# Phase weight loaded by SyncE, two-token loads for five groups, seven block products in two pairs instead of three, and another order of steps

## The chip, the cores and the metric

The kernel runs on one core of a Trainium2 chip. The metric is the device time of one execution in microseconds (us). TensorE (PE) multiplies and transposes, VectorE (DVE) and ScalarE (ACT) move and change what PE wrote, GpSimd (POOL) and SyncE (SP) mostly start DMA transfers.

## The reference, cut to what matters

q, k and v are (8, 8, 576, 64): batch, heads, tokens, head dimension. Attention is local to chunks of 64 tokens. Its output x (8, 576, 512) goes through a mixing layer with four weights.

```python
def _attn_ref(q, k, v):
    ...                                   # chunks of 64 tokens
    scores = scale * np.matmul(q_c, k_c.transpose(0, 1, 2, 4, 3))
    ...
    attn = np.exp(scores)
    attn = attn / (np.sum(attn, axis=-1, keepdims=True) + 1e-09)
    out = np.matmul(attn, v_c)

def _moe_ref(x, w_theta, w_tok_r, w_tok_i, w_ch):
    theta = x @ w_theta
    cos_t, sin_t = (np.cos(theta), np.sin(theta))
    zr = x * cos_t
    zi = x * sin_t
    yr = np.einsum('ts,bsd->btd', w_tok_r, zr)
    yi = np.einsum('ts,bsd->btd', w_tok_i, zi)
    y = yr + yi
    u = x + y
    return (u + np.maximum(u @ w_ch, 0.0)).astype(np.float32)
```

## The kernel before, in words

The batches are taken two at a time, as pairs 0 to 3. The 2 x 576 tokens of a pair are nine tiles of 128, in five groups: A and B hold the first 512 tokens of the pair's first batch (two tiles each), C and D those of its second, and M is one tile with the last 64 tokens of both.

Nothing is scheduled by a program. `ORDER` is a list of steps, and each engine does its instructions in the order of that list. A step reads `kind.pairGroup.bank`: `H.0D.2` is the projection of group D of pair 0 into PSUM bank 2. A digit at the end of a kind is a half of the step (one tile of two, or one half of the heads); halves 2 and 3 are halves of the columns of the first tile. The kinds that matter here:

- `qF`, `kF` (line 181): POOL's load of q or k, cast to fp16, four tokens to a partition, so 64 partitions hold a group. `q`, `k` (lines 194 and 208): two tokens to a partition for a group of two tiles, 128 partitions; plain rows for M. `v` (lines 222, 232): v, in two or three transfers.
- `lt`, `lc`, `lw` (lines 251, 254, 243): the phase weight w_theta, the channel weight w_ch, and the token weights in parts.
- `F` (line 301, 128 transposes of 64x64), `FL` (line 316, 32 transposes of 128 columns), `L` (line 339, 32 of 128 columns for a group of two tiles), `N` (line 335): PE transposes q and k. `tq`, `tk` copy them to SBUF (`V` and `A` in these and other names: by VectorE or ScalarE).
- `S` scores, `e` exp, `V` attention times v, `n` normalisation (lines 405, 422, 440, 452 and 454): x of a group.
- `X`, `Q` (lines 478, 487): transposes of x; `xA`, `xV` their copy; `H` (line 518): x times w_theta; `g` cos and sin; `z` the products zr and zi on VectorE.
- `TW`, `tw`: transposes of the token weights and their copy.
- `Y` (lines 590, 604): token mixing done directly. A group of a batch takes nine products to a tile. `YA` to `YM` do the part of it that comes from one group. `y` (line 723) adds x and makes u.
- `K` (line 693) with `j` (line 653) and `r` (line 712): token mixing of A to D of both batches by seven block products in place of eight. `j` takes differences of z on VectorE, `jw` sums of the weight blocks; `r` adds a product from PSUM to x, eight times for a pair.
- `U`, `R`, `uA`, `uV`, `W` (line 518 again), `w` (line 733), `s`, `sA`: u is transposed, copied, multiplied by w_ch, relu and u are added, and the result is stored by SyncE's or ScalarE's queue.
- `D` fills PE at the start with products of zeros; `pe`, `pg` load ScalarE's table for exp or sine.

Pair 0 uses `Y` (its parts by group), pairs 1 to 3 use `K` for A to D and `Y` for M. Loads of pairs 1 to 3 pass `gate`: POOL waits until the latest normalisation named before them in `ORDER` has run. The q and k tiles, the token weights, the differences of z and the later output tiles share one pool of ten buffers (`nat`).

Of the kernel before, what the change touches and what calls it, by code (L numbers as in the profile page):

```python
# [9 lines left out]
FP32 = mybir.dt.float32  # L10
# [12 lines left out]
n0.0C n1.0C H1.0A.7 H0.0A.6 v.0B V1.0B.0 n1.0B v.0M lw.02 Q.0C.4 xA.0C g1.0A V0.0M.2 n0.0M g0.0A
V0.0B.0 V1.0M.3 H.0C.4 lw.00 qF.1C kF.1C n0.0B X0.0B.0 n1.0M qF.1A kF.1A X1.0B.1 z.0D xV1.0B
Q.0M.2 xA.0M qF.1B kF.1B v.1C TW.02.6 twV.02 H.0M.3 g.0C TW.03.1 twA.03 q.1M k.1M xV0.0B z1.0A
z.0C H1.0B.0 v.1A g.0M z0.0A qF.2A v.1D TW.01.6 twV.01 H0.0B.1 g0.0B z.0M TW.00.4 F.1C.3.2 tq.1C
twA.00 jw.00 YD.0D.6 g1.0B z1.0B YC.0D.6 F.1A.0.1 tkA.1C S.1C.2 pe.00 e.1C YM.0C.4 tq.1A YM.0D.6
y.0D YC.0C.4 tkA.1A z0.0B F.1B.0.1 qF.1D kF.1D V0.1C.2 v.1B S.1A.6 lw.04 tq.1B YD.0C.4 e.1A y.0C
n0.1C kF.2A lc.00 tkA.1B YA.0A.6 V1.1A.0 n1.1A V0.1A.4 YB.0A.6 v.1M V1.1C.0 n0.1A S.1B.2 L.1M.4
qF.2C e.1B X.1A.5 qF.2D xA.1A n1.1C X.1C.0 kF.2C YM.0A.6 U.0D.1 H.1A.2 xV.1C pg.00 g.1A tq.1M  # L30
uV.0D H.1C.0 tkV.1M kF.2D F.1D.5.4 tkA.1D y.0A jw.01 v.2A R.0C.6 g.1C tq.1D uV.0C YA.0B.2 S.1D.4
V0.1B.6 YM.0B.2 n0.1B z.1C YB.0B.2 e.1D y.0B FL.2A.0 qF.2B tqA.2A V1.1D.6 q.2M V0.1D.4 n0.1D
W.0D.2 S.1M.4 k.2M n1.1D w.0D X.1D.6 kF.2B TW.04.7 tkA.2A e.1M v.2D twV.04 V1.1M.0 V0.1M.1
S.2A.2 xA.1D e.2A V1.1B.4 n1.1B n0.1M z.1A H.1D.6 n1.1M X.1B.5 pg.00 g.1D xV.1B W.0C.2 w.0C
ja.1C R.0A.0 X.1M.4 uA.0A sA.0C z.1D qF.3A jc.1D U.0B.5 H.1B.6 uA.0B v.2C g.1B xA.1M W.0A.0
Ka.1A.2 w.0A F.2C.4.5 F.2D.0.1 ra.1A tq.2D tkA.2C tkA.2D sA.0D jb.1D qF.3D Y.0M.7 V0.2A.0 n0.2A
z.1B tqA.2C H.1M.6 y.0M N.2M.4 tkA.2M g.1M Kf.1C.2 S.2D.0 tqA.2M F.2B.7.6 V1.2A.4 rc.1C n1.2A
z.1M v.3D e.2D tqA.2B kF.3D Kg.1D.2 rg.1B X.2A.0 xV.2A Ke.1C.4 re.1D tkA.2B v.2M Km.1D.2 qF.3B
U.0M.1 rf.1D H.2A.6 pg.00 g.2A uV.0M Kc.1D.4 jd.1B S.2C.0 pe.00 e.2C q.3M v.2B s.0A rd.1C
V0.2D.6 n0.2D Y.1M.2 S.2B.6 kF.3A y.1M V0.2C.0 n0.2C e.2B k.3M Kb.1B.4 z.2A V1.2C.6 qF.3C kF.3C  # L40
S.2M.0 e.2M n1.2C W.0B.2 rb.1A V1.2D.0 n1.2D Q.2C.6 W.0M.4 U.1C.5 w.0B s.0B v.3A w.0M U.1A.0
uV.1C X.2D.1 xA.2C H.2C.2 xV.2D V1.2M.4 V0.2B.6 uA.1A V0.2M.5 pg.00 g.2C n1.2M n0.2B H.2D.0
W.1A.6 g.2D n0.2M Q.2M.4 xA.2M F.3A.2.3 F.3D.0.1 z.2C w.1A V1.2B.4 n1.2B tkA.3D W.1C.6 tqA.3A
ja.2C z.2D X.2B.1 w.1C H.2M.2 xA.2B Kd.1B.4 tkA.3A tqA.3D g.2M H.2B.6 rh.1B v.3C s.0M S.3A.0
jb.2D kF.3B R.1D.2 Ka.2A.4 g.2B v.3B Ke.2C.6 z.2M uA.1D ra.2A Kf.2C.4 F.3C.2.3 e.3A V0.3A.0
jc.2D tkA.3C re.2D n0.3A tqA.3C rc.2C Kc.2D.6 rd.2C V1.3A.0 n1.3A S.3D.2 e.3D Kg.2D.4 z.2B rg.2B
S.3C.6 s.1A e.3C Q.3A.0 W.1D.2 U.1B.6 v.3M Km.2D.4 xA.3A H.3A.0 w.1D rf.2D V0.3C.2 n0.3C R.1M.4
uV.1M uA.1B W.1B.6 sA.1C jd.2B F.3B.2.3 N.3M.4 pg.00 g.3A z.3A w.1B Kb.2B.0 tqA.3B tkA.3B
V1.3C.2 tqA.3M rb.2A S.3B.6 pe.00 e.3B Y.2M.5 n1.3C tkV.3M Q.3C.0 xA.3C V0.3D.6 y.2M n0.3D
S.3M.2 W.1M.4 e.3M w.1M U.2C.5 uA.2C V1.3D.0 V1.3M.2 n1.3D s.1B V0.3M.3 n0.3M n1.3M H.3C.6 pg.00  # L50
g.3C V0.3B.0 sA.1M Q.3D.4 xV.3D Kd.2B.2 n0.3B rh.2B V1.3B.0 n1.3B R.2D.6 uA.2D W.2C.4 w.2C
Q.3B.0 xV.3B R.2B.6 z.3C uA.2B H.3D.2 g.3D R.2A.0 ja.3C uA.2A Q.3M.6 xA.3M z.3D jb.3D H.3B.4
# [9 lines left out]
def kernel(  # L62
# [22 lines left out]
    GT = 2 * P  # L85
# [20 lines left out]
    nat = ctx.enter_context(tc.tile_pool(name="nat", bufs=10))  # L106
# [60 lines left out]
    def gate(p):  # L167

        if p and marks:
            nc.gpsimd.tensor_copy(out=seen, in_=marks.pop())  # L170
            marks.clear()

    def load_qk(p, g, which, plain, f=None):
        j0, bb, s0 = GROUPS[g]
        gate(p)
        if (p, g) not in nats:
            nats[p, g] = nat.tile([P, 2, 2 * DM], FP16, name="qk16", tag="nat")
        if plain is None:
# [560 lines left out]
    def store(p, g, f, queue):  # L739
# [71 lines left out]
    with tc.manual_schedule():  # L811
        for step in ORDER:
# [5 lines left out]
            p, g = int(at[0]), int(at[1]) if at[1].isdigit() else at[1]  # L818
# [36 lines left out]
```

## Time and profile before

| | us |
|---|---|
| time, median of 3 runs | 203.94 (202.31 to 204.08) |
| the profiled execution: time | 205.1 |
| the profiled execution: span | 203.3 |
| PE busy | 186.4 (92%) |
| VectorE busy | 150.3 (74%) |
| ScalarE busy | 124.4 (61%) |
| POOL busy, mostly starting transfers | 83.3 (41%) |
| last matmul ends | 197.9 |
| mean granted PE clock | 0.999 |

The span runs from the first to the last instruction of the profiled execution; its time is 1.8 us longer. Matmuls overlap in PE's pipeline, so a group's mean (380 ns for a 128x512 matmul) isn't what one of them adds to the time: in the chain of waits eight of them take about 1.8 us.

### The profile page before, as it was taken

The page shows a single profiled execution, that of the slowest core. Times are in us where ns is not written, and L with a number is a line of the kernel's source. Part 1 is how long each engine was busy: PE and PEld are TensorE (multiplying, and loading weights), DVE is VectorE, ACT ScalarE, POOL GpSimd, SP SyncE. Part 2 cuts the span into 40 slices and gives each one's busy share as a digit, 9 for nine tenths or more (in the row PEclk, how much of TensorE's full clock was granted, in tenths as well). Part 3 has the DMA queues.
Part 4 walks back from the last instruction along what each step waited for, and adds up shares of the span by engine and source line. Part 5 has one row for each costly group of instructions (what it writes and reads, how often), then busy time and mean ns, then how long its engine had stood idle before and what let it go on. Part 6 is the DMA issues. An engine that isn't in the chain of part 4 may idle for free.

```text
span 203.3 us, 7900 instructions
## 1 busy us (share of the span) xinstructions
PE 186.4 (92%) x3567; PEld 99.6 (49%) x3567; DVE 150.3 (74%) x238; ACT 124.4 (61%) x150; POOL 83.3 (41%) x134
## 2 busy tenths in 40 slices
PE   7677587999989979999999999999999999999990
PEld 2345445555455545555455564455555544445530
DVE  0042738975766869989988888979988899889480
ACT  2354577995168869679673978956889366001510
POOL 7875957749959675105956137002000000000000
PEclk9999999999999999999999999999999999999999
DMA  5999999999999999962999929505121002004875
GB/s 62 177 191 146 157 141 196 195 175 121 167 178 182 175 128 104 221 223 23 136 141 129 228 108 124 34 3 77 59 106 41 19 3 103 0 0 157 298 286 194
DMA packets 70433, 26.48 MB, mean 130 GB/s; under 512 B 47232, under 2 KB 65792, under 8 KB 70400
## 3 DMA queue, kind: packets, MB, share of 16 engines
q0 software_dynamic: 65408, 16.54, 85.9%
q10 hardware_dynamic: 2496, 4.72, 6.5%
q1 hardware_dynamic: 2496, 4.72, 6.4%
q8 instruction: 28, 0.46, 0.9%
q14 instruction: 5, 0.04, 0.1%
HBM read 33.06 MB, written 9.44 MB: 209 GB/s over the span
## 4 chain that ended last, share of the span: by engine, by line
PE 84%; DMA 4%; POOL 3%; issue 3%; ACT 2%; DVE 1%; ACTq 0%; POOLq 0%
PE ps L518 32%; PE ps L693 21%; PE ps L604 8%; DMA qk<-in_k_dram 4%; PE ps L590 4%; PE ps L478 4%; PE ps L440 3%; PE ps L301 3%; PE ps L487 3%; PE ps L405 3%; POOL qk L181 2%; PE ps L269 2%; POOL v L232 1%; ACT kT L372 1%; PE ps L316 1%
## 5 line engine op out<-in xcount | busy, mean ns | idle before, releaser
L232 POOL DMA_DIRECT2D v<-in_v_dram x48 | 36.3, 778 | 3.6 <-DMA qk<-in_k_dram 2.0
L518 PE MATMUL ps<-wch,uT 128*128 128x512 f16 x144 | 34.1, 380 | 1.2 <-issue 1.2
L518 PE MATMUL ps<-wtheta,xT 128*128 128x512 f16 x144 | 34.5, 380 | 0.0
L712 DVE TENSOR_TENSOR x<-ps,x 128x1024 f16<-128x1024 f32 x24 | 29.1, 1221 | 4.6 <-PE ps L693 4.1
L501 ACT COPY uT<-ps 128x1024 f16<-128x1024 f16 (+1 forms) x14 | 13.6, 982 | 25.8 <-PE ps L487 18.7
L733 DVE SCALAR_TENSOR_TENSOR o<-ps,x 128x1024 f32<-128x1024 f32 (+1 forms) x20 | 22.2, 1115 | 6.7 <-PE ps L518 6.4
L454 DVE TENSOR_TENSOR x<-ps,recip 128x512 f16<-128x512 f32 (+1 forms) x40 | 25.5, 638 | 1.4
L532 ACT ACTIVATE cos<-ps,pihalf 128x1024 f16<-128x1024 f32 (+1 forms) x22 | 21.1, 959 | 6.8 <-PE ps L518 5.8
L422 ACT ACTIVATE eT<-ps 128x1024 f16<-128x1024 f32 (+1 forms) x18 | 16.5, 926 | 11.5 <-PE ps L405 11.2
L372 ACT COPY kT<-ps 128x1024 f16<-128x1024 f16 (+1 forms) x18 | 16.3, 922 | 9.6 <-PE ps L301 5.5
L518 PEld LDWEIGHTS <-uT 128*128 128x128 f16 x144 | 13.1, 98 | 16.2 <-issue 1.7
L518 PEld LDWEIGHTS <-xT 128*128 128x128 f16 x144 | 12.9, 98 | 13.6
L536 ACT ACTIVATE sin<-ps 128x1024 f16<-128x1024 f32 (+1 forms) x22 | 19.0, 865 | 0.0
L693 PE MATMUL ps<-z,wT 128*128 128x512 f16 x72 | 18.8, 379 | 0.0
L170 POOL COPY seen<-recip 1x1 f32<-1x1 f32 x16 | 3.2, 199 | 37.4 <-DVE recip L452 37.4
L452 DVE RECIPROCAL recip<-ps 128x8 f32<-128x8 f32 (+1 forms) x40 | 7.9, 198 | 12.7 <-PE ps L440 11.9
L604 PE MATMUL ps<-z,wT 128*128 128x512 f16 x72 | 16.9, 380 | 0.1
L368 DVE COPY qT<-ps 128x1024 f16<-128x1024 f16 (+2 forms) x11 | 6.4, 581 | 14.3 <-PE ps L316 9.3
L693 PE MATMUL ps<-zsum,wsum 128*128 128x512 f16 x72 | 16.7, 379 | 0.2 <-DVE x L712 0.2
L693 PEld LDWEIGHTS <-wsum 128*128 128x128 f16 x96 | 9.1, 98 | 10.5 <-issue 0.2
L693 PEld LDWEIGHTS <-wT 128*128 128x128 f16 x96 | 9.1, 98 | 10.3
L370 ACT COPY qT<-ps 128x1024 f16<-128x1024 f16 (+2 forms) x12 | 9.9, 823 | 6.5 <-PE ps L316 5.8
(68 smaller groups left out, 294.3 us busy)
## 6 DMA issues: line engine op xcount, KB each, us to landing
qk<-in_q_dram POOLq DMA_DIRECT2D x16, 256.0 KB, 6.0
qk<-in_k_dram POOLq DMA_DIRECT2D x16, 256.0 KB, 6.7
out_dram<-o ACTq DMA_DIRECT2D x8, 512.0 KB, 4.9
out_dram<-o SPq DMA_DIRECT2D x8, 512.0 KB, 3.7
v<-in_v_dram POOLq DMA_DIRECT2D x40, 64.0 KB, 5.3
v<-in_v_dram POOLq DMA_DIRECT2D x16, 128.0 KB, 5.7
wnat<-in_moe_w_tok_r_dram POOLq DMA_DIRECT2D x2, 288.0 KB, 5.8
wnat<-in_moe_w_tok_i_dram POOLq DMA_DIRECT2D x2, 288.0 KB, 6.3
```

The source lines that it names most:

```text
L232: nc.gpsimd.dma_start(v16[rows, slot + tile, :, 0:D], v[2 * p + bb, :, t0 : t0 + m, :].rearrange("h s d -> s h d"),)
L372: nc.scalar.copy(out=t.rearrange("p x s c -> p x (s c)").rearrange("p x (c s) -> p x c s", s=n), in_=ps.rearrange("p x s c -> p x c s"),)
L422: nc.scalar.activation(out=eT.rearrange("p h r e c -> p (h r e) c"), in_=ps, func=AF.Exp, scale=scale)
L454: nc.vector.tensor_tensor(out=tokens(p, g, "x")[:, :, f * NE * D : (f + 1) * NE * D].rearrange("p c (h d) -> p c h d", h=NE), in0=psv[:, 0 ...
L501: (nc.vector.tensor_copy if how == "V" else nc.scalar.copy)(out=to.rearrange("p b (r c) -> p b r c", c=CH), in_=psv)
L518: nc.tensor.matmul(ps[:, a * DM : a * DM + cols.stop - cols.start], xT[:, b0 + a, db, :], weight[:, db, cols], start=(db == 0), stop=(db = ...
L532: nc.scalar.activation(out=cos[:, 0:n].rearrange("p a e -> p (a e)"), in_=pin, func=AF.Sin, bias=pihalf, scale=1.0,)
L536: nc.scalar.activation(out=sin[:, 0:n].rearrange("p a e -> p (a e)"), in_=pin, func=AF.Sin)
L604: nc.tensor.matmul(ps[:, a * DM : a * DM + DM], wT[:, kt, t0 : t0 + P], zs[bb], start=(done + k == 0), stop=(done + k == NK - 1),)
L693: nc.tensor.matmul(ps[:, a * DM : a * DM + DM], wt, zt, start=fresh and i == 0, stop=i == len(terms) - 1, skip_group_check=to in ("x", "z"),)
L712: nc.vector.tensor_tensor(out=u, in0=st[p]["ps_k", frm], in1=u, op=ALU.add)
L733: nc.vector.scalar_tensor_tensor(out=o, in0=ps[:, 0 : n * m].rearrange("p (j d) -> p j d", j=n), scalar=0.0, in1=u, op0=ALU.max, op1=ALU.add,)
```

## The change

The phase weight is loaded in two fp32 halves by SyncE's queue and cast to fp16 by VectorE (`ctV`, new), instead of one casting load by POOL. Both halves use buffers of the pool `nat`. Groups B, A, C, D of pair 0 and A of pair 1 are loaded with two tokens to a partition (`q`, `k`) and transposed by `L`, for 0B and 0A in halves; M is transposed by `N`. Pairs 1 and 2 use the seven block products; pair 3 uses `Y`, its groups C and D a tile at a time. The order of nearly all steps is another: it begins with 0B, 0M and 0A (the first batch of pair 0), the direct token mixing of that batch begins before group D is transposed, and the last tile of all goes through `W`, `w` and the store in two halves of 256 columns.

```diff
@@ ORDER, cut to the beginning and the end @@
-qF.0A kF.0A id.00 init.00 D.12.0 qF.0D D.5.0 FL1.0A.0 kF.0D FL0.0A.2 tqA1.0A tq0.0A tkA1.0A
-S1.0A.0 tkA0.0A F.0D.7.6 tq.0D tkA.0D D.5.2 S.0D.2 e1.0A S0.0A.4 e0.0A v.0A qF.0C D.2.0 V0.0A.0
-qF.0B V1.0A.4 n0.0A kF.0B D.6.0 FL0.0B.0 e.0D FL1.0B.2 kF.0C F.0C.6.7 tkA0.0B tqA0.0B n1.0A
-X1.0A.4 tkA.0C tq1.0B v.0D X0.0A.5 D.3.0 V0.0D.0 tq.0C q.0M k.0M n0.0D lt.00 xV0.0A tkA1.0B
-S1.0B.2 V1.0D.6 n1.0D e1.0B S.0C.0 L0.0M.2 L1.0M.3 e.0C tkV0.0M tkV1.0M X.0D.5 xV.0D tq1.0M
-tqA0.0M S0.0B.0 e0.0B S0.0M.6 S1.0M.0 e1.0M H.0D.2 xV1.0A e0.0M v.0C V0.0C.0 V1.0C.4 pg.00 g.0D
...
-uA.3B sA.1D U.3M.4 uA.3D W.3D.2 s.3A w.3D W.3B.0 sA.3C R.2M.2 sA.3D uV.3M w.3B s.3B W.3M.4 w.3M
-s.3M uA.2M W.2M.7 w.2M sA.2M
+q.0B k.0B init.00 D.12.0 lt.00 ctV1.00 ctV0.00 q.0M k.0M id.00 D.15.0 L0.0B.0.1 tkA0.0B
+L1.0B.7.6 tq1.0B N0.0M.1 tkV0.0M tkA1.0B q.0A N1.0M.2 tq0.0B S1.0B.6 tkV1.0M tq0.0M S0.0M.0
+e1.0B tq1.0M S0.0B.6 v.0B D.5.2 V1.0B.2 e0.0B e0.0M V0.0B.0 n0.0B k.0A S1.0M.4 D.3.6 L1.0A.6.7
+v.0M n1.0B L0.0A.0.1 tq1.0A e1.0M Q0.0B.2 tq0.0A tkA1.0A S1.0A.4 Q1.0B.6 tkA0.0A S0.0A.0 e1.0A
+e0.0A V1.0M.4 xV1.0B v.0A V0.0M.5 xV0.0B V1.0A.6 n1.0A V0.0A.0 lw.00 n0.0A H0.0B.3 pg.00 g0.0B
+H1.0B.6 X1.0A.7 X0.0A.0 xA0.0A xA1.0A n1.0M g1.0B TW.00.2 H0.0A.4 g0.0A n0.0M X.0M.0 xV.0M
+TW.01.6 z0.0B H1.0A.0 H.0M.1 twA.01 q.0C z1.0B k.0C L.0C.4.5 twV.00 YB.0A.2 z0.0A g1.0A z1.0A
+g.0M tq.0C YA.0A.2 lw.02 z.0M tkA.0C TW.02.0 YM.0A.2 S.0C.4 pe.00 e.0C twV.02 q.1A k.1A y.0A
+L.1A.7.6 TW.03.0 tkA.1A q.0D k.0D v.0C L.0D.2.3 tqA.0D v.0D qF.1B twV.03 lc.00 tkA.0D kF.1B
+qF.2D kF.2D qF.1D YM.0B.4 YA.0B.4 v.1A tq.1A kF.1D S.0D.6 e.0D V0.0C.0 n0.0C v.1D V1.0C.2 n1.0C
+YB.0B.4 y.0B U.0A.0 uA.0A V1.0D.6 S.1A.2 X.0C.1 xA.0C n1.0D FL.1B.4 tq.1B qF.1C kF.1C V0.0D.6
+H.0C.0 n0.0D q.1M X.0D.6 e.1A xV.0D jw.00 tkA.1B g.0C W.0A.2 w.0A z.0C H.0D.6 g.0D FL.1D.0 tq.1D
...
+V0.3D.5 n0.3D H.3A.2 g.3A R.2D.6 uV.2D Q.3M.0 xV.3M W.2B.4 sA.1D V0.3C.6 n0.3C R.2C.0 W.2D.2
+uA.2C V1.3C.0 w.2B Q.3D.6 xA.3D w.2D W.2C.4 sA.2B H.3M.2 n1.3C R.2A.0 s.2M w.2C z.3A Q.3C.6
+xA.3C H.3D.4 H.3C.6 sA.2C sA.2D z.3B g.3M z.3M Y.3B.2 y.3B uV.2A g.3D z.3D Y.3A.4 y.3A g.3C z.3C
+W.2A.0 s.1A Y0.3D.2 w.2A s.2A Y.3M.3 R.3B.0 y0.3D R0.3D.4 R.3A.6 y.3M uV.3B uV.3A s.1M Y0.3C.2
+y0.3C W.3B.6 uA0.3D W0.3D.0 W.3A.4 w.3A U.3M.1 Y1.3C.2 w.3B sA.3A uA.3M Y1.3D.3 s.3B y1.3C
+U1.3C.1 W.3M.2 w0.3D y1.3D w.3M s0.3D R0.3C.6 uV0.3C uA1.3C R1.3D.0 W1.3C.3 uA1.3D W1.3D.0 w1.3C
+w1.3D sA.3M sA1.3C W3.3C.7 w3.3C W2.3C.1 s1.3D s3.3C w2.3C s2.3C
@@
+    wraw = []
     wnat = {}
@@
     def load_theta():
-        nc.gpsimd.dma_start(wtheta16, moe_w_theta.rearrange("(a p) e -> p a e", p=P))
+        for a in range(2):
+            t = nat.tile([P, 2, DM], FP32, name="wraw", tag="nat")
+            wraw.append(t)
+            nc.sync.dma_start(
+                t, moe_w_theta[a * GT : a * GT + GT, :].rearrange("(a p) e -> p a e", p=P)
+            )
+
+    def cast_theta(a, copy):
+        copy(out=wtheta16[:, 2 * a : 2 * a + 2], in_=wraw[a])
@@
+        "ctA": lambda p, g, f: cast_theta(f, nc.scalar.copy),
+        "ctV": lambda p, g, f: cast_theta(f, nc.vector.tensor_copy),
```

More of the change, by code (lines that the diff above doesn't have):

```diff
@@ L23 @@
[L23 to L52, printed above, removed]
@@ L53 @@
-Ka.3A.2 ra.3A H.3M.0 g.3M z.3M Ke.3C.6 Kf.3C.2 sA.2C re.3D rc.3C W.2A.0 g.3B z.3B w.2A Kc.3D.6
-rd.3C W.2D.4 w.2D jc.3D Kb.3B.0 W.2B.4 jd.3B Kg.3D.2 rb.3A Kd.3B.0 rg.3B Km.3D.2 w.2B R.3A.6
-rh.3B s.2B Y.3M.4 rf.3D s.2A y.3M uA.3A sA.2D R.3C.0 R.3D.2 R.3B.6 W.3A.4 uA.3C w.3A W.3C.0 w.3C
-uA.3B sA.1D U.3M.4 uA.3D W.3D.2 s.3A w.3D W.3B.0 sA.3C R.2M.2 sA.3D uV.3M w.3B s.3B W.3M.4 w.3M
-s.3M uA.2M W.2M.7 w.2M sA.2M
+q.0B k.0B init.00 D.12.0 lt.00 ctV1.00 ctV0.00 q.0M k.0M id.00 D.15.0 L0.0B.0.1 tkA0.0B
@@ new lines @@
+g.0M tq.0C YA.0A.2 lw.02 z.0M tkA.0C TW.02.0 YM.0A.2 S.0C.4 pe.00 e.0C twV.02 q.1A k.1A y.0A
[3 more added lines that the diff above has]
+H.0C.0 n0.0D q.1M X.0D.6 e.1A xV.0D jw.00 tkA.1B g.0C W.0A.2 w.0A z.0C H.0D.6 g.0D FL.1D.0 tq.1D
+U.0B.2 qF.2A YC.0C.4 uV.0B tkA.1D v.1M k.1M S.1D.6 V0.1A.0 z.0D V1.1A.2 YM.0C.4 YD.0C.4 v.1C
@@ new lines @@
+pe.00 e.1D V0.1D.6 n0.1A S.1B.0 e.1B n1.1A y.0C FL.1C.2 tqA.1C lw.04 V1.1D.4 tkA.1C U.0C.0 qF.2B
+n0.1D kF.2B X.1A.1 uV.0C xV.1A W.0B.6 v.1B n1.1D S.1C.0 Q.1D.2 xV.1D H.1A.4 e.1C V1.1C.0 V0.1C.2
+v.2B pg.00 g.1A w.0B H.1D.6 n1.1C qF.2C n0.1C TW.04.0 g.1D jw.01 kF.2C kF.2A z.1A FL.2D.2 tkA.2D
+N.1M.1 X.1C.4 YD.0D.6 xV.1C tkV.1M v.2A YM.0D.6 v.2C tqA.2D twV.04 tq.1M S.1M.0 S.2D.2 V0.1B.4
+n0.1B pe.00 e.1M z.1D YC.0D.6 e.2D q.2M y.0D H.1C.0 pg.00 g.1C s.0A V1.1M.2 F.2C.3.4 V1.1B.6
+V0.1M.5 n1.1M Y.0M.2 n0.1M tqA.2C U.0D.5 tkA.2C W.0C.0 uA.0D qF.3B n1.1B z.1C y.0M ja.1C X.1M.2
@@ new lines @@
+xV.1M w.0C F.2A.7.6 v.3A jb.1D tqA.2A FL.2B.4 jc.1D W.0D.2 tqA.2B w.0D H.1M.7 Ka.1A.0 X.1B.2
+tkA.2A tkA.2B g.1M U.0M.3 ra.1A v.2D S.2A.4 pe.00 e.2A uV.0M S.2C.6 xV.1B Kf.1C.0 e.2C V0.2A.2
+v.2M z.1M V0.2D.4 s.0B k.2M H.1B.6 pg.00 g.1B v.3D n0.2D Ke.1C.4 n0.2A rc.1C V1.2A.2 n1.2A
+Kg.1D.0 S.2B.2 V0.2C.6 re.1D kF.3B Kc.1D.4 pe.00 e.2B z.1B v.3M qF.3D N.2M.2 tqA.2M tkA.2M v.3B
+n0.2C rg.1B V1.2C.6 Y.1M.3 qF.3A n1.2C s.0D rd.1C V1.2B.6 n1.2B X.2C.2 X.2A.4 xA.2A xA.2C qF.3C
+kF.3C Km.1D.0 Kb.1B.6 S.2M.4 rf.1D V1.2D.0 y.1M H.2A.2 e.2M rb.1A V0.2B.4 V1.2M.6 n1.2D pg.00
@@ new lines @@
+g.2A V0.2M.7 n0.2B U.1C.0 uV.1C X.2D.1 X.2B.5 xV.2B kF.3D W.0M.4 w.0M xA.2D H.2C.2 n0.2M H.2D.0
+s.0C g.2C n1.2M kF.3A X.2M.7 s.0M xA.2M g.2D z.2A H.2B.4 jd.1B Kd.1B.6 H.2M.0 z.2C ja.2C g.2B
+rh.1B F.3B.1.2 z.2D F.3A.3.4 tkA.3B tqA.3B Ke.2C.6 z.2B re.2D U.1B.5 tkA.3A jb.2D W.1C.1 w.1C
+uA.1B g.2M tqA.3A W.1B.4 z.2M R.1A.0 uA.1A Ka.2A.2 Kc.2D.6 S.3B.0 pe.00 e.3B w.1B ra.2A S.3A.4
+e.3A Kf.2C.2 q.3M jc.2D U.1D.0 jd.2B W.1A.4 rc.2C uV.1D Kg.2D.2 k.3M rd.2C w.1A rg.2B U.1M.0
+uA.1M F.3C.1.7 V0.3B.4 Y.2M.6 n0.3B y.2M tqA.3C tkA.3C Km.2D.2 V1.3B.0 n1.3B rf.2D S.3C.4 s.1C
@@ new lines @@
+e.3C Kb.2B.6 rb.2A U.2M.0 N.3M.1 tkA.3M F.3D.2.3 tqA.3M v.3C V1.3A.4 n1.3A W.1D.6 tq.3D tkA.3D
+S.3D.4 V0.3A.2 n0.3A uA.2M Kd.2B.0 S.3M.2 w.1D Q.3B.6 e.3D e.3M rh.2B s.1B W.1M.5 w.1M V1.3M.2
+n1.3M Q.3A.0 R.2B.3 xA.3B V1.3D.6 n1.3D W.2M.5 w.2M xA.3A H.3B.0 uV.2B pg.00 g.3B V0.3M.7 n0.3M
+V0.3D.5 n0.3D H.3A.2 g.3A R.2D.6 uV.2D Q.3M.0 xV.3M W.2B.4 sA.1D V0.3C.6 n0.3C R.2C.0 W.2D.2
+uA.2C V1.3C.0 w.2B Q.3D.6 xA.3D w.2D W.2C.4 sA.2B H.3M.2 n1.3C R.2A.0 s.2M w.2C z.3A Q.3C.6
+xA.3C H.3D.4 H.3C.6 sA.2C sA.2D z.3B g.3M z.3M Y.3B.2 y.3B uV.2A g.3D z.3D Y.3A.4 y.3A g.3C z.3C
```

## The prediction

> **What bounds the kernel now.** The page comes first: TensorE (PE) is busy 92% of the span, and the slices show where the rest is. The first three tenths-digits are low and the last is 0; between them PE is nearly full. The DMA row is full for the first 28 slices (140 us).
>
> ```profile
> PE 186.4 (92%) x3567; PEld 99.6 (49%) x3567; DVE 150.3 (74%) x238; ACT 124.4 (61%) x150; POOL 83.3 (41%) x134
> ...
> PE   7677587999989979999999999999999999999990
> ...
> DMA  5999999999999999962999929505121002004875
> ```
>
> Second, the chain of waits in order of time. Its pieces are start, length, what. It leaves the loads at 17.0 us; the first projection (x times the phase weight, L518) starts at 25.39, and from there to 197.92 the chain is PE but for ten small pieces.
>
> ```profile
> 8.18 8.83 DMA qk<-in_k_dram
> ...
> 25.39 1.83 PE ps L518 x8
> ...
> 48.63 0.64 PE ps L301 x64
> ...
> 49.70 3.56 PE ps L604 x16
> ...
> 55.98 0.57 PE ps L339 x16
> ...
> 58.03 0.81 issue
> ...
> 68.38 1.01 PE ps L316 x32
> ...
> 71.39 1.21 issue
> ...
> 92.00 1.24 DVE x L712
> ...
> 136.00 1.83 PE ps L693 x8
> ...
> 197.94 0.69 DVE o L733
> ```
>
> Summed by line from 25.3 to 197.92, the pieces give 167.1 us of PE work and 5.3 us of gaps (3.2 issue, 2.1 waits for VectorE). Divided by the instructions that ran in that stretch, a line's sum is its unit price, with what little is lost between steps inside it: L518 64.75/288 = 225 ns, L604 227, L693 42.16/192 = 220, the 64x64 transposes of L301 8.7 (6.12/704), the 128-column ones of L316 31.6 and L339 35.6, L335 62.5, L478 61 (7.57/124), L487 9.7 (5.71/592), L405 9.1, L440 12.9. So the span is 25.3 of start, 167.1 of PE, 5.3 of gaps and 5.4 after the last matmul: 203.1, beside 203.3. Neither VectorE nor ScalarE sets the end; only what moves one of these four terms counts.
>
> Third, the DMA view in windows of one microsecond, for the start. At 5 to 6 us the four-token loads of q and k run (packets that write 512 B), at 24 to 25 us those of v (128 B):
>
> ```profile
> DMA packets 385, 0.20 MB, mean 195 GB/s; under 512 B 4, under 2 KB 385, under 8 KB 385
> ```
> ```profile
> DMA packets 1215, 0.15 MB, mean 153 GB/s; under 512 B 1214, under 2 KB 1215, under 8 KB 1215
> ```
>
> So a four-token load (512 packets) takes 1.33 us of the stream, the v of a group (2048 small packets, at about 1180/us over several such windows) 1.74, the v, q or k of a middle tile 0.87. Over the first 25 us these sum to nearly what went by: the start is a full DMA stream.
>
> **The start, changed.** POOL's queue now asks for 0B, 0M, 0A, and the first projection is H0.0B, behind V0.0A, which needs v.0A. The phase weight goes by SyncE in fp32: 1.05 MB instead of POOL's one load (2.7 us of stream at 0.20 MB/us, at 21 to 23 us). Where SyncE's queue and POOL's ran together, at 86 to 88 us, they moved 327 GB/s, so I take 3.2 us, between 2.8 (375 GB/s among the last stores) and 3.9 (270). I count all of it ahead of the first groups' loads, since it goes out in the same microseconds as q.0B and shares their engines. The two-token load, 1024 packets that write 256 B, isn't in the trace. Bounds: 1.33 us, if bytes decide as between 512 B and 1 KB (0.20 MB/us both), and 2.66, if a packet costs what a 512 B one does. The 128 B and 512 B rows, 0.85 and 2.6 ns a packet, put 256 B on their line at 1.43 ns, or 1.46 us: I take 1.45, as both neighbours are measured. Stream to v.0A: first packets 2.9 + 3.2 + four q and k loads 5.8 + q, k of 0M 1.74 + v.0B 1.74 + v.0M 0.87 + v.0A 1.74 = 18.0. A landing is seen about 1 us after its last packet (qF.0A and kF.0A: 2.9 + 2.7, used at 6.8), and V1.0A and V0.0A take 0.5: H0.0B at 19.5 instead of 25.3, **-5.8 us** (-6.7 to -0.3 by the bounds: four loads at 1.33 to 2.66, the weight at 2.8 to 3.9). POOL issues a load in 0.7 us, so the 16 up to v.0A take some 12 us and stay ahead of the stream; SyncE has nothing else until the first store.
>
> The two casts of the weight stand first in VectorE's queue after the memsets, ahead of tq1.0B. Nearest rows for 128x1024: 0.69 (f16 copy) to 1.22 (fp32 add). The weight has landed by some 8 us, so they end at 9.4 to 10.5, beside tq1.0B at about 10. What hides a late one is v.0B, which lands at 14.6; without that cover it would cost 1 us.
>
> The Trainium skill's page "DMA: Bandwidth & Descriptors", section Specifications, speaks against this edit: below 512 B a transfer leaves line rate and is read, modified and written. Here 128 B packets lose only a quarter of the bytes per microsecond (0.15 beside 0.20 MB). Taken as half of line rate the rule would price a load at 2.7 us, and the sum below would gain 12 us; by the rows it gains nothing.
>
> **PE work after the first projection.** Counts by line from both kernels' instruction order.
> - Pair 3 loses 64 product matmuls (L693, 14.05 us) and gets 72 direct ones (L604, 16.33): +2.3.
> - q and k transposes. Before: 704 L301, 32 L316, 16 L339, 16 L335 = 8.7 us. After: 384, 160, 96, 24 = 3.3 + 5.1 + 3.4 + 1.5 = 13.3: +4.6, in part since 0C and 0D now come behind the first projection.
> - x and u transposes: 44 more of L478 (+2.7), 144 fewer of L487 (-1.4): +1.3.
> - scores and attention: +56 of L405, -16 of L440: +0.3.
> Together **+8.5 us**: 175.6.
>
> VectorE loses 8 product adds (9.8 us) and 4 differences (4.9), gains 6 adds (5.2), two casts, and 6 uT copies (4.1) that leave ScalarE: about 4 us less of 150. ScalarE loses some 4. Both lie beside PE and I count nothing; the cover is the PE chain itself.
>
> **Gaps.** PE has 28.8 us of work between H0.0B and FL.1D, so reaches it at 48.3. The stream has 31.2 us between v.0A and kF.1D (two token-weight loads 6.4, six two-token loads 8.7, v 0C, 0D, 1A 5.2, six four-token loads 8.0, the last weight 2.9), so that lands at 50.2: PE waits 1.9. The gaps of before in as long a stretch after its first projection are 2.0, which such a wait would swallow. So I take the old 5.3 in all; the ends are 1.9 (that wait alone) and twice the old, 10.6.
>
> **The end.** Before, the last add takes 0.69, two stores are issued (1.16), and 256 KB goes out: 5.4 us. After, the last piece has 256 columns: the add about 0.42 (row of the 128x256 TENSOR_TENSOR), one issue (0.55) and half the bytes (at 0.3 MB/us, 0.4 less): -1.3, so 4.1. Earlier stores go out while PE still works.
>
> **Sum.** 19.5 + 175.6 + 5.3 + 4.1 = 204.5, against 203.3: +1.2. The profiled execution took 205.1 with its 1.8 around the span, 1.2 over the median of the runs, 203.94. So 203.94 + 1.2 = **205.1 us**. Three runs of this kernel spread 0.9%, so about 1% (2.0 us) can be told from no change.
>
> **Rivals.** (1) Slower: small packets. If a two-token load costs d more than 1.45 us, ten of them lie before kF.1D and PE's end is 50.2 + 10d + 146.8 (PE work left) + 3.3 (the later gaps) = 200.3 + 10d, beside 200.4 in the sum: it decides from the first tenth, and from d = 0.1 the kernel is over 1% slower. At d = 0.45 the time is 209.5; at the upper bound, 1.21, 217. For it: the load exists in no row, and POOL also has to start twice the packets. Against: bytes per microsecond fall slowly from 512 to 128 B. The skill's line-rate rule above is this rival's upper end.
>
> (2) Slower: Y.3B waits for z.3M. From n0.3C on, PE has 11.3 us until Y.3B's ninth matmul needs z.3M; VectorE has 9.9 us queued through z.3M (two norms 1.8, three w 3.7, z.3A, z.3B and z.3M 4.4), and g.3M stands on ScalarE behind the stores sA.2C and sA.2D, so ends at about 9.3. Any wait over 1 us of ScalarE there reaches PE. The waits of before have one of 4.7:
>
> ```profile
> ACT uT L501 <- DMA out_dram<-o: 4.7, 1, 4.7
> ```
>
> In that size it costs 4.0: 209.1. Against: the o tiles of both stores are ready in time by the sum, and the stores of before's last 18 us were denser.
>
> (3) Faster: the gaps shrink. PE has 6516 rows instead of 7136, VectorE and ScalarE have less to do, and the 2.1 us of waits for VectorE belong to steps that are gone or moved. With 1.9 of gaps the span is 201.1: **201.7 us**; with the stream's lower bounds as well, about 200. Against: the issue gaps fall where DMA is full (27 to 73 us), and it stays so.
>
> That the weight's move brings nothing would need H0.0B at 25.3, 1.45 more for each of four loads, above the upper bound; at most part of (1).
>
> **Chances.** The sum as it stands, within 1%: 0.38. Rival 1: 0.22, rival 2 or a like wait near the end: 0.18, both slower by over 1%; rival 3: 0.22, faster. So faster 0.22, same 0.38, slower 0.40. The range takes rival 3 with part of the lower bounds and rivals 1 and 2 to d = 0.45: 200.5 to 209.5. The likeliest case alone is 203.5 to 206.0.
>
> **What would show it.** First L518 at 19.5 (not over 21); packets of 256 B at about 700 per us; the wait ahead of FL.1D (the second group of L316) near 2 us; PE pieces after the first projection 175 to 176; no wait of ScalarE before g.3M; 4 us after the last matmul. Wrong would be a first projection after 23, PE work under 172 or over 179, or gaps under 2 or over 10.

## The result

The changed kernel takes 206.40 us (median of 20 runs, 204.16 to 209.68) beside 203.94 (20 runs, 201.76 to 208.15). The ratio is **1.0104, with a 95% interval of 1.0070 to 1.0138**: about 1% slower. Disturbed executions are left out of the ratios here and below, but not out of the medians and spreads. A second set of runs (in the experiments) gave 1.0184 [1.0111, 1.0258], and the kernel before measured against itself 0.9938 [0.9904, 0.9973], so a ratio within some 0.6% of 1 says nothing by itself, whatever its interval.

The profiled execution of the changed kernel took 204.54 us, 1.9 under its median, while that of the kernel before, 205.1, was 1.2 over its own. The two spans, 202.7 and 203.3, therefore stand the wrong way round by 0.6 us, and the profile shows what such an execution is made of, not the whole difference of the medians.

The page of the changed kernel, busy times and slices (one digit is a fortieth of the span, some 5 us):

```profile
span 202.7 us, 7306 instructions
...
PE 193.7 (96%) x3257; PEld 104.9 (52%) x3257; DVE 144.9 (71%) x243; ACT 120.3 (59%) x148; POOL 85.8 (42%) x135
...
PE   7977999999899999999999999999999999999992
...
PEclk9999699999999999999999999999999999999998
DMA  6999999999999999999897990500802525004076
```

PE is fuller at the start, where it had 7677587, and its clock has a 6 in the fifth slice, which the kernel before did not have. VectorE is busy 5.4 us less and ScalarE 4.1 less. DMA is near full for the first 24 slices, 122 us, where it was 140.

The chain of waits in order of time (start, length, what):

```profile
9.63 4.92 DMA v<-in_v_dram
...
17.64 0.81 issue
...
19.98 3.33 PE ps L527 x8
...
28.79 1.01 PE ps L348 x32
29.80 3.56 PE ps L613 x16
...
42.79 8.79 DMA qk<-in_k_dram
51.62 1.08 PE ps L325 x32
...
169.71 7.77 PE ps L613 x36
...
198.49 0.40 DVE o L742
```

L527 is the old L518 and L613 the old L604; L325 and L348 are L316 and L339. The first projection starts at 19.98 in place of 25.39, but its eight matmuls take 3.33 us in place of 1.83. A load of k, which did not stand in the chain this late before, now reaches down to L325. The last stretch is products of L613 where L693 stood.

The timeline of PE, the places where it waited or ran slow (start, length, line, tile; in brackets the idle time before it and what ended that):

```profile
18.45 0.29 PE L496 MATMUL ps<-id,x 64*64 64x64 f16 x13 [0.81 <-issue]
19.34 0.64 PE L449 MATMUL ps<-v,eT 64*64 64x65 f16 x32 [0.22 <-DVE xT L510]
19.91 3.40 PE L527 MATMUL ps<-wtheta,xT 128*128 128x512 f16 x8
...
44.02 1.08 PE L325 MATMUL ps<-id,qk 128*64 128x128 f16 x32 [0.24 <-DMA qk<-in_k_dram]
...
51.62 1.08 PE L325 MATMUL ps<-id,qk 128*64 128x128 f16 x32 [0.53 <-DMA qk<-in_k_dram]
...
195.88 2.77 PE L527 MATMUL ps<-wch,uT 128*128 128x512 f16 x16
```

From 19.91 to the end of the last matmul at 198.65 are 178.7 us. Of these, 1.5 are the slow first projection (3.40; in other executions below it takes 1.90) and 1.35 are the waits over 0.2 us (0.30 for ScalarE at 26.2, the two above, and 0.28 at 76.5 for another k). That leaves 175.9 of work, small gaps included. After 77 us PE has no wait over 0.2.

### The profile page after: what moved, and what is told of

Its sections match the earlier page's. It is cut to its first block, busy times and chain, and to the rows that moved or that the text cites. A ratio compares the mean times of both kernels' runs of the same rounds, so it can differ in the third digit from the quotient of the medians.

```text
span 202.7 us, 7306 instructions
## 1 busy us (share of the span) xinstructions
PE 193.7 (96%) x3257; PEld 104.9 (52%) x3257; DVE 144.9 (71%) x243; ACT 120.3 (59%) x148; POOL 85.8 (42%) x135
## 4 chain that ended last, share of the span: by engine, by line
PE 71%; DMA 12%; POOL 9%; issue 3%; DVE 1%; ACT 1%; DVEq 0%; POOLq 0%
PE ps L527 24%; PE ps L702 14%; PE ps L613 12%; DMA qk<-in_k_dram 8%; PE ps L599 4%; POOL v L233 4%; PE ps L487 4%; PE ps L449 3%; DMA v<-in_v_dram 2%; PE ps L496 2%; PE ps L414 2%; PE ps L310 2%; PE ps L325 2%; PE ps L348 1%; POOL qk L209 1%
## 5 line engine op out<-in xcount | busy, mean ns | idle before, releaser
L527 PE MATMUL ps<-wtheta,xT 128*128 128x512 f16 x144 | 35.6, 392 | 0.1
L527 PE MATMUL ps<-wch,uT 128*128 128x512 f16 (+1 forms) x148 | 33.9, 374 | 0.0
L613 PE MATMUL ps<-z,wT 128*128 128x512 f16 x144 | 33.1, 380 | 0.0
L742 DVE SCALAR_TENSOR_TENSOR o<-ps,x 128x1024 f32<-128x1024 f32 (+2 forms) x23 | 22.5, 988 | 5.4 <-PE ps L527 5.3
L510 ACT COPY uT<-ps 128x512 f16<-128x512 f16 (+1 forms) x11 | 8.6, 782 | 29.6 <-PE ps L496 13.8
L721 DVE TENSOR_TENSOR x<-ps,x 128x1024 f16<-128x1024 f32 x16 | 19.5, 1220 | 4.7 <-PE ps L702 4.6
L527 PEld LDWEIGHTS <-xT 128*128 128x128 f16 x144 | 13.5, 100 | 15.8 <-issue 1.4
L613 PEld LDWEIGHTS <-wT 128*128 128x128 f16 x144 | 13.4, 98 | 15.0
L527 PEld LDWEIGHTS <-uT 128*128 128x128 f16 x148 | 13.5, 98 | 13.7 <-ACT uT L510 0.3
L732 DVE TENSOR_TENSOR x<-ps,x 128x512 f16<-128x512 f32 (+1 forms) x14 | 12.8, 918 | 9.0 <-PE ps L613 6.4
L545 ACT ACTIVATE sin<-ps 128x1024 f16<-128x1024 f32 (+1 forms) x22 | 19.2, 872 | 0.0
L510 ACT COPY xT<-ps 128x1024 f16<-128x1024 f16 (+1 forms) x11 | 9.6, 894 | 7.6 <-PE ps L496 3.9
L487 PE MATMUL ps<-id,x 128*128 128x128 f16 x168 | 13.0, 222 | 0.0
L487 PEld LDWEIGHTS <-x 128*128 128x128 f16 x168 | 10.8, 99 | 4.1 <-issue 1.0
```

Source lines behind the costliest of these rows:

```text
L487: nc.tensor.transpose(psv[:, b].rearrange("p r c -> p (r c)"), x[:, a0 + j, a * P : a * P + P], id16,)
L510: (nc.vector.tensor_copy if how == "V" else nc.scalar.copy)(out=to.rearrange("p b (r c) -> p b r c", c=CH), in_=psv)
L527: nc.tensor.matmul(ps[:, a * DM : a * DM + cols.stop - cols.start], xT[:, b0 + a, db, :], weight[:, db, cols], start=(db == 0), stop=(db = ...
L545: nc.scalar.activation(out=sin[:, 0:n].rearrange("p a e -> p (a e)"), in_=pin, func=AF.Sin)
L613: nc.tensor.matmul(ps[:, a * DM : a * DM + DM], wT[:, kt, t0 : t0 + P], zs[bb], start=(done + k == 0), stop=(done + k == NK - 1),)
L721: nc.vector.tensor_tensor(out=u, in0=st[p]["ps_k", frm], in1=u, op=ALU.add)
```

## The experiments

Theories: (A) the sum stands, the extra work of pair 3 and of the transposes (+8.5) eats the early start (-5.4) and the shorter tail (-1.3), and little else matters; (B) the rest of the loss is the clock, halved while the first projection runs; (C) it is the loads, which have no slack once PE starts 5 us sooner; (D) it is PE's own instruction loading, the "issue" gaps.

**The kernel before once more.** No edit.

> The kernel before, unchanged, for a second profile and the clocks of its executions. If the 3.2 us of PE gaps named issue belong to the kernel, they stand again at the same four places after the first projection; if they belong to the execution, they move or shrink to under 1.5 us. If the changed kernel loses its time to half-speed windows of the PE clock, this kernel shows a granted clock of 0.995 or more in most executions; if the clock has no part in it, its clocks spread as widely (0.97 to 1.00) as those of the changed kernel do.

202.93 us, ratio 0.9938 [0.9904, 0.9973], profiled at a span of 199.8. Of the four issue gaps after the first projection in the profile before (0.55, 0.43, 0.81 and 1.21 us, from 28 to 73 us) this is left:

```profile
27.88 0.42 PE L440 MATMUL ps<-v,eT 64*64 64x65 f16 x28 [0.28 <-issue]
```

So the 3.2 us of issue gaps that the sum carried over (the chain counts small pieces too) belong to that execution as much as to the kernel. The granted clocks of its nine executions spread from 0.981 to 0.999, those of the changed kernel's twenty from 0.971 to 1.000: the kernel before loses clock too.

**Eight more products with zeros, to keep the clock up.**

```diff
-Q0.0B.2 ... Q1.0B.6
+D.4.2 Q0.0B.2 ... D.4.6 Q1.0B.6
```

> The changed kernel with eight more products of zeros on PE, four ahead of each half of Q.0B, in the 3.4 us of small transposes before the first projection. Theory of the clock: a window of small products counts as idle and the next one, in which the projections run, is granted half speed; with the dummies the clock is 0.995 or more, H0.0B takes 0.97 us instead of up to 2, and the median falls from 206.4 to 204 to 205, a ratio to before of about 1.003. Rival, PE work: the lost clock is hidden behind the wait for the load kF.1D, the dummies add up to 1.7 us ahead of H0.0B, and the ratio stays at 1.010 or grows.

206.56 us, 1.0120 [1.0087, 1.0153]: no faster than the changed kernel. The clock was at full speed throughout the profile, but the eight products put the first projection off by 1.4 us; it took 1.90 in place of 3.40 and so ended at 23.2, as in the changed kernel (23.3). What the clock gave, the products took, and at 45 us PE met a load of k again:

```profile
21.34 1.90 PE L526 MATMUL ps<-wtheta,xT 128*128 128x512 f16 x8
...
45.54 1.08 PE L324 MATMUL ps<-id,qk 128*64 128x128 f16 x32 [1.28 <-DMA qk<-in_k_dram]
```

So the run does not say what the half clock costs, only that full speed bought with eight products gains nothing. The wait of 1.28 us for kF.1B is the first sign for C. Theory B stays open. Of the changed kernel's executions that the ratio counts, five were granted 0.996 or more and took 204.16 to 205.22 us, four 0.980 to 0.983 and took 206.44 to 206.90. A low clock goes with a longer time there; whether it is the cause, or follows from a wait for a load, these numbers can't tell. Here five of six were granted 1.000 and took 205.59 to 207.31, so a full clock alone does not make the time short.

**Four-token loads and the 64x64 transposes (`F`) for the five groups**, which undoes that part of the change alone.

```diff
-q.0B k.0B ... L0.0B.0.1 ... L.0C.4.5
+qF.0B kF.0B ... F0.0B.0.1 ... F.0C.4.5
```

> The changed kernel with the four-token loads and the 64x64 transposes for the five groups too. Theory of PE work: each group's transposes cost 0.56 instead of 1.14 us, 1.7 us in all after the first projection, and ten loads of 1.33 instead of 1.45 bring kF.1D 1.2 us earlier; the time falls by 1.7 to 2.5 us, a ratio to before of 0.998 to 1.002. Theory of the clock: it stays within 0.7 us of the changed kernel (1.007 to 1.014), with clocks of 0.97 to 1.00, since 64x64 transposes count for even less activity ahead of H0.0B.

216.02 us, 1.0454 [1.0400, 1.0508]. Both expectations missed, by 6 to 10 us. The profiled execution took 215.84 us, the shortest of the six 212.41. (`F` takes 64 transposes of 64x64 for q and k of a group together, not the 128 of the list of steps: 832 rows for 13 groups in the kernel before.) No load was late behind the first projection; PE stood still for 11.8 us in seven gaps that nothing in the kernel explains, among them:

```profile
22.89 0.38 PE L448 MATMUL ps<-v,eT 64*64 64x65 f16 x13 [3.01 <-issue]
...
46.07 0.44 PE L448 MATMUL ps<-v,eT 64*64 64x65 f16 x17 [2.35 <-issue]
...
88.55 0.19 PE L448 MATMUL ps<-v,eT 64*64 64x65 f16 x1 [2.56 <-issue]
```

The profile has one more queue beside those of the data: the instruction queue, 16 KB to a packet, 26 packets in this kernel, 28 before and 25 after. Their number goes with PE's instructions: 6834, 7134 and 6514 of PE and PEld, some 260 to a packet. Read in windows of 0.1 us, a packet of it begins at 20.4, 43.6 and 85.6, that is 2.5, 2.5 and 2.9 us before PE goes on after the three gaps above; the other four gaps end 2.5 to 2.8 us after packets at 14.5, 36.8, 50.5 and 65.9. The window 20.4 to 20.5:

```profile
q8 instruction: 1, 0.02, 55.4%
```

The gaps of the other profiles fit as well: before, packets at 56.3 and 69.7 and PE goes on at 58.84 and 72.60; after, 15.8 and 18.45. So I read an issue gap as PE waiting for its next block of instructions, which shares the 16 DMA engines with the loads. The coincidence in time is shown; the next pair tests whether the number of instructions is the cause.

**The same four-token loads with 128-column transposes (`FL`)**, 32 instructions to a group instead of 64.

```diff
-q.0B k.0B ... L1.0B.7.6 ... L.0C.4.5
+qF.0B kF.0B ... FL1.0B.6 ... FL.0C.4
```

> The changed kernel with four-token loads for the five groups, but transposed by 32 instructions of 128 columns (L316) as the two-token ones are (L339), not by 64 of 64x64. Theory of instruction fetch: the 10 us that the 64x64 transposes cost came from their instructions alone, so this stays with the changed kernel or gains a little (0.4 us of PE work, 1.2 us of the load stream): ratio to before 1.002 to 1.010. Rival, the four-token loads themselves are slow (64 partitions): ratio 1.03 or more.

204.60 us, 1.0024 [0.9984, 1.0063]: some 9 us less than with `F` by the ratios (11 by the medians), with the same loads and groups. Its profile has no issue gap over 0.2 us, and one wait that counts, again for kF.1B:

```profile
43.27 1.08 PE L324 MATMUL ps<-id,qk 128*64 128x128 f16 x32 [1.16 <-DMA qk<-in_k_dram]
```

So the 64x64 transposes made that kernel slow, not the loads, and D is the reading that fits: the issue gaps went with half of the transposes' instructions. No run changed the instruction queue by itself. The run also shows that the two tokens to a partition cost time: without them the kernel is level with the one before, against 1.0184 [1.0111, 1.0258] for the changed kernel in the same set of runs and 1.0104 in the first. By the prices of the prediction they cost 1.6 us (ten loads at 0.12 each, and 96 transposes dearer by 4 ns); the runs give 1.6 to 3.3, and 1.1 in the later pair of load orders, whose intervals overlap.

**The 128-column transposes in the kernel before**, for 0C, 0D, 1A, 1B, 1C and 1D.

```diff
-F.0D.7.6 ... F.0C.6.7 ... F.1C.3.2 ... F.1A.0.1
+FL.0D.6 ... FL.0C.6 ... FL.1C.2 ... FL.1A.0
```

> The kernel before with the longer transposes (L316, 32 instructions) in place of 64 of 64x64 for the six groups 0D, 0C, 1C, 1A, 1B, 1D, whose loads and all else stay. By the unit prices alone, 31.6 beside 8.7 ns, each costs 0.45 us more: 2.7 in all, ratio 1.013. Theory of instruction fetch: the issue gaps between 21 and 73 us (3 to 4 us) shrink to under 1, and the ratio is 0.994 to 1.003.

203.64 us, 1.0022 [0.9985, 1.0059]. No issue gap over 0.2 us is left in its profile after the first projection. PE is busy 189.3 us, 2.9 and 3.6 more than in the two profiles of the kernel before, so the work priced at +2.7 is there, but it does not show in the time. That dearer, but fewer instructions cancel fits D; the repeat of the kernel before had few issue gaps without them, so it is not proof.

**The direct mixing in pair 3 of the kernel before**, that part of the change alone.

```diff
-H.3B.4 Ka.3A.2 ra.3A H.3M.0 ... Km.3D.2 ... rf.3D ...
+H.3B.4 H.3M.0 g.3M z.3M Y.3C.6 sA.2C W.2A.0 g.3B z.3B y.3C ... Y.3B.2 y.3A s.2B y.3B R.3A.6 Y.3M.4 s.2A y.3M
```

> The kernel before with the direct mixing for pair 3 alone (72 matmuls of L604 for 64 of L693, no differences of z, four adds of u for eight), all else as before. Theory of PE work: PE is full there, so it costs 16.3 - 14.1 = 2.3 us, ratio 1.011. Rival: VectorE, freed of 10 us, and the shorter chain give it back, ratio 0.998 to 1.003.

206.61 us, 1.0121 [1.0087, 1.0154], so 2.5 us. The term was +2.3, and PE is busy 188.4 us, 2.0 and 2.7 more than in the two profiles of the kernel before: the term is shown, and this part is a loss by itself. That the time agrees to 0.2 us is in part luck, since the profile also has two waits in this stretch that the price does not hold:

```profile
164.92 1.04 PE L515 MATMUL ps<-wtheta,xT 128*128 128x512 f16 x4 [1.17 <-ACT xT L498]
...
168.54 2.32 PE L601 MATMUL ps<-z,wT 128*128 128x512 f16 x10 [0.86 <-DVE z L553]
```

**The changed kernel once more.** No edit.

> The changed kernel, unchanged, for a second profile beside the others of this call. Theory of instruction fetch (PE's issue gaps end about 1.65 us after a 16 KB block of the instruction queue has landed, so they come where many small matmuls meet a full DMA stream): its issue gaps after the first projection are under 1.5 us in all, since the 32 longer transposes of a group are half as many instructions; the ratio to before is 1.007 to 1.014 again. Rival, that the gaps are chance of the execution: 3 us or more of them.

207.58 us, 1.0184 [1.0111, 1.0258]; the profiled execution took 207.79, its span is 205.8. Here the first projection ran at full clock (20.62, 1.90 us), no issue gap over 0.2 us stands behind it, as the theory of instruction fetch had it, and the ratio is above the 1.007 to 1.014 expected. The main difference to the first profile is one wait:

```profile
46.54 1.75 PE L325 MATMUL ps<-id,qk 128*64 128x128 f16 x32 [3.73 <-DMA qk<-in_k_dram]
```

After it the clock is halved until about 50: 1.75 for these 32 instead of 1.08, and 2.66 for the next eight of L527 instead of 1.90. The last matmul ends at 201.76; less the waits (0.30 and 3.73) and 1.4 of half clock, 175.7 us of work are left, beside 175.9. What was late is the stream. The DMA view of 40 to 45 us, first in the first profile, then in this one:

```profile
DMA packets 1706, 0.89 MB, mean 179 GB/s; under 512 B 53, under 2 KB 1706, under 8 KB 1706
```
```profile
DMA packets 1268, 0.78 MB, mean 156 GB/s; under 512 B 36, under 2 KB 1267, under 8 KB 1267
```

The same list of loads moved 12% fewer bytes in those 5 us, and as much fewer in the 5 before (0.71 beside 0.81 MB). POOL also issued kF.1B 1.3 us later, at 36.40 beside 35.11, which is half of its delay. PE met its wait at 43.8 in the one and 42.8 in the other, so kF.1B was there at 44.0 or at 46.5.

**The loads for 1B and 1D sooner**, to test C: kF.1B ahead of the channel weight, and the two loads of 2D behind kF.1C.

```diff
-lc.00 tkA.0D kF.1B qF.2D kF.2D qF.1D
+kF.1B tkA.0D lc.00 qF.1D
...
-qF.1C kF.1C V0.0D.6
+qF.1C kF.1C qF.2D kF.2D V0.0D.6
```

> The changed kernel with three loads moved in POOL's queue alone: kF.1B ahead of the channel weight, and q and k of 2D (used some 20 us later) behind k of 1C, so that kF.1B comes 2.9 us and kF.1D 2.7 us earlier in the stream. Theory that the change left the load stream no slack, so that an execution with a slower stream waits at FL.1B or FL.1D (0.8 us in one profile, 3.7 in the other): the waits there go to under 0.5 us, and the ratio to before falls from 1.010 to 1.018 in two measurements to 0.998 to 1.005. Rival, PE work alone: the loss is the 8.5 us of added transposes and products, and the ratio stays at 1.008 or more.

206.49 us, 1.0065 [1.0014, 1.0115], between the two expectations. In the profile (span 201.3) the two waits are gone; the largest left for a load is

```profile
75.14 0.69 PE L309 MATMUL ps<-id,qk 64*64 64x64 f16 x62 [0.57 <-DMA qk<-in_k_dram]
```

The best runs show the gain (203.18, the changed kernel never under 204.16), the median does not, and the runs still reach to 209.5. The intervals of this ratio and of the changed kernel's overlap. C is right for the profiles: the waits went with the move. Whether it is all of what the medians lose is not settled.

**The phase weight by POOL's casting load again**, at the same place in the order, without the casts.

```diff
-            nc.sync.dma_start(t, moe_w_theta[...])   # two halves, fp32, then ctV
+        nc.gpsimd.dma_start(wtheta16, moe_w_theta.rearrange("(a p) e -> p a e", p=P))
```

> The changed kernel with the phase weight loaded by POOL in one casting load at the same place of the order, without the casts on VectorE. Theory that the order of the loads makes the early start and the queue does not: the stream to v.0A is 2.7 instead of 3.2 us for the weight, the first projection is within 1 us of 19.9, ratio 1.006 to 1.013. Rival, SyncE's queue makes it, since its packets go out before POOL's first: the first projection comes at 22 us or later, ratio 1.018 or more.

206.96 us, 1.0168 [1.0106, 1.0230]: not to be told from the changed kernel. Yet the first projection comes 2.6 and 1.9 us later than in the two profiles of the changed kernel:

```profile
22.50 1.90 PE L520 MATMUL ps<-wtheta,xT 128*128 128x512 f16 x8
```

Its one wait for a load of k behind that is 0.8, for kF.1D. So by these profiles SyncE's queue does bring the start forward. That what it brings is lost again where PE meets the loads of 1B and 1D fits them (waits and half clock of 2.9 and 5.4 us in the two profiles of the changed kernel, 1.1 here), but is argued from one profile.

**Both mends together**: the load order, and the four-token loads with 128-column transposes.

```diff
+ the edits of "the loads sooner" and of "128-column transposes" to the changed kernel
```

> The last kernel with the four-token loads and 128-column transposes of the five groups as well. By the prices of the prediction that is 1.2 us of the stream and 0.4 us of PE work less: if the stream no longer binds, 0.4 us (ratio 0.996 to 1.003, the same as without it); if it still does, 1.5 us more than that.

204.24 us, 1.0013 [0.9960, 1.0065]. Level with the kernel before, as without the new load order (1.0024). There the order of the loads adds nothing that can be measured.

**The same with seven block products in pair 3**, in a new order for the end.

```diff
-Y.3B.2 y.3B uV.2A ... Y0.3D.2 ... Y1.3C.2 ... w2.3C s2.3C
+Ka.3A.2 ra.3A uV.2A g.3D z.3D Kb.3B.4 rb.3A ... Km.3D.2 rf.3D ... W2.3D.7 w2.3D s2.3D
```

> The four-long kernel with the loads moved, and pair 3 by the seven block products again, in an end of the order written for it (Ka and Kb while z of C is made). Theory of PE work: 64 products of L693 instead of 72 of L604, 2.3 us less than the kernel without it, ratio to before 0.984 to 0.992. Rival: the differences of z and the eight adds stand in VectorE's way at the end, where the direct mixing had none, and the ratio is 0.996 or more.

207.30 us, 1.0161 [1.0098, 1.0223]: 2.3 less was hoped for, 3 more came. By the profile the lower product count is lost to VectorE, which must add the partial products before PE can go on; four waits near the end (0.36, 0.33, 0.49, 0.94), the last of them

```profile
193.16 0.59 PE L701 MATMUL ps<-z,wT 128*128 128x512 f16 x2 [0.94 <-DVE x L720]
```

and one of 1.83 at 57 us, in a part of the order that the edit left alone, which stays unexplained. My order for the end is not as good as the one it replaces; the run says what that order costs, not what the seven products could give in a better one.

None of these kernels is measurably faster than the kernel before.

## Why the prediction was right, and where it was not

Forecast: 204.5 of span, 205.1 us, 1.2 over the kernel before. Measured: 206.40 us, 2.5 over by the medians, 2.1 by the ratio. That lies inside the range of 200.5 to 209.5, but above the 203.5 to 206.0 of the likeliest case.

The terms, measured on PE's own timeline in two profiles of each kernel. A wait counts from 0.2 us on, half clock is what slow matmuls took beyond their time at full clock, and work is the rest up to the last matmul:

| term | predicted | before | before again | changed | changed again |
|---|---|---|---|---|---|
| first projection starts | 19.5 | 25.3 | 25.6 | 19.9 | 20.6 |
| PE work after it | 175.6 | 168.7 | 168.0 | 175.9 | 175.7 |
| half clock | none | none | none | 1.5 | 1.4 |
| gaps and waits | 5.3 | 3.9 | 1.2 | 1.35 | 4.0 |
| after the last matmul | 4.1 | 5.4 | 5.1 | 4.05 | 4.05 |
| span | 204.5 | 203.3 | 199.8 | 202.7 | 205.8 |

*The start* was right within 0.4 and 1.1 us, and for the reason given: the three loads of v.0A landed between 18.9 and 19.6 us (19.2 and 20.0 in the second profile), where the sum had 19.0. The chain names other things at its last steps, an issue gap of 0.81 us (1.23 in the second profile) and a copy of x by VectorE, which ends at 19.3 beside those landings. So PE's own path was about as long as the loads', which the sum did not count. Two-token loads were put at 1.43 ns a packet, about 700 packets per us. The DMA view of 29 to 30 us, in which only such packets run:

```profile
DMA packets 717, 0.18 MB, mean 181 GB/s; under 512 B 717, under 2 KB 717, under 8 KB 717
```

1024 packets take 1.43 us at that rate. Rival 1 (small packets dearer) is out. The line-rate rule of the Trainium skill's page "DMA: Bandwidth & Descriptors", section Specifications, which was that rival's upper end, is not borne out as a factor: 195, 181 and 153 GB/s at 512, 256 and 128 B are a slow fall. (These are bytes written; the source is fp32, so twice as many are read.) The weight by SyncE went at 0.31 to 0.37 MB a microsecond from 2 to 5 us, about the rate taken, and its casts ended at 7.1, far ahead of the first use:

```profile
DMA packets 199, 0.37 MB, mean 375 GB/s; under 512 B 16, under 2 KB 16, under 8 KB 199
```
```profile
5.47 1.62 DVE L260 CAST wtheta<-wraw 128x1024 f16<-128x1024 f32 x2 [3.68 <-DMA wraw<-in_moe_w_theta_dram]
```

*PE work* came out right in total, in part by luck. The prediction took 167.1 us of work and 5.3 of gaps from the chain of waits before. The chain has pieces of VectorE there (0.22, 0.70 and 1.24 us, 2.1 in all) while PE itself waited for VectorE only 0.65 and 0.25 us, and worked on in the rest. PE's timeline gives 168.7 of work and 3.9 of waits in the same profile. Against that the work grew by 7.0 to 7.9 us, where +8.5 was counted. Counting instructions by line and multiplying by unit prices had the direction and most of the size; pair 3 was confirmed by its own run. *The end* was right to 0.05 us. *Rival 2* (Y.3B waits for z.3M) did not come: PE has no wait over 0.2 us there, and ScalarE none for an output store.

*The gaps* are the step that failed, in three ways that partly offset. Gaps under 2 were named as a sign of being wrong, and the first profile has 1.35. First, I kept the old 5.3, of which 3.2 were issue gaps. These are no constant of a kernel: 3.2 us in the profile before, 0.3 in its repeat, none over 0.2 us behind the first projection in either profile of the changed kernel. Rival 3 had this right, but not the time that it gave. Second, the wait for the loads of 1B and 1D was put at 1.9, ahead of FL.1D. It came at FL.1B, one group sooner, as well, and its size is not one number: 0.24 at FL.1B and 0.53 at FL.1D in the first profile, 3.73 and nothing in the second. Third, the half clock was put at nothing: 1.4 to 1.5 us in both profiles, at different places.

*VectorE and ScalarE* were to lose some 4 us each and lost 5.4 and 4.1. In the first profile PE has no wait over 0.2 us for VectorE behind the first projection, and one of 0.30 for ScalarE.

Why then slower by more than the 1.2 of the forecast? In the means of the two profiles of each kernel, start, work and tail give -5.2 + 7.5 - 1.2 = +1.1; the forecast had -5.8 + 8.5 - 1.3 = +1.4. Half clock adds 1.5 and the waits 0.1, together 2.7, where the two sets of runs give 2.1 and 3.7 by their ratios. But the four pairs of spans differ by -0.6 to 6.0 us, so two profiles of each can't fix a single term. The mechanism of the forecast, an early start paid for with PE work, was right. What it lacked are load waits and a slow clock, which stand where the issue gaps stood. Why the same list of loads moves 12% fewer bytes in one execution than in another stays open; no run here set it, and the run that took the wait out of the profile took only part of the loss out of the median.

## What to carry to other kernels

When work starts sooner, ask at once which load is met next: here 5 us were won at the first projection, and in the profiles PE then waited for a load of k that had not been in its way, for 0.24 us in one execution and 3.73 in another. Count PE's instructions as well as their time while the load stream is full: half as many transposes at over three times the price of one were some 9 us faster in one order and not measurably slower in another. Take work and gaps from one account: the chain of waits counted as gaps what PE's own timeline has as work. A gap or a wait in a profile is one draw: take it into a sum only after a second execution of the same kernel has shown it too.

## What the runs showed of the hardware

- Instruction blocks travel over the same DMA engines as data (16 KB packets on their own queue), and PE had issue gaps that go with them: up to 3.0 us at a time, 11.8 us in one execution, PE going on each time 2.4 to 3.0 us after a block began. The kernel with 64 small transposes to each early group under a full stream had most of them, those with 32 to a group few or none behind the first projection. That PE stood still for the block is the reading that fits; it is not shown by itself.
- The clock was halved after 16 to 20 us, in which PE was busy 2.86 of 4 us with 64x64 matmuls, and was not halved after the same stretch in the second profile, with 2.46 of 4. There it was halved after a wait of 3.73 us. The Trainium skill's page "TensorE: Matmul & The Clock Gate", section "What's actually happening", has the clock at half after an idle window of about 3.4 us; the long wait agrees (0.50 of full clock from 48 to 50 us), the first case, without an idle stretch of that length, the trace does not explain. In the kernel before with 128-column transposes a wait of 2.37 us, ending at 11.27, was enough (0.50 from 12 to 14 us). The windows of the first profile that show it, with the busy time of PE, PEld, VectorE, ScalarE and POOL, then the clock, the DMA share and GB/s:

```profile
20.00:22.00 2.00, 2.00 (x6) 0.76 (x7) 1.90 (x6) 1.46 (x3) 0.00 (x0) 0.54 1.73 183
22.00:24.00 2.00, 2.00 (x17) 1.19 (x14) 0.74 (x3) 0.84 (x3) 1.26 (x3) 0.61 1.58 197
```

- Lost clock can hide behind a load: in the first profile 1.5 us were lost at 20 us, and PE still waited 0.24 us for kF.1B at 44. That the load would have come no sooner at full clock is argued, not run.
